# Which weight blocks a recurrent attention loop streams: one key block kept, a sixth output block streamed

## The chip, the core and the metric

The kernel runs on one core of a Trainium2 chip. The metric is the device time of the whole kernel in microseconds. Three runs before the change took 2378.48, 2380.43 and 2387.71 us; the median is 2380.43. The profiled execution spans 2380.4 us at a mean granted TensorE clock of 0.97.

## The reference

Two independent parts are computed and joined along the last axis. Part B is a long convolution over 2048 positions and 1024 channels; nothing of it is touched here. Part A is an attention layer with a recurrent memory, and it fixes the order of the work:

```python
for s in range(n_seg):                       # 64 segments of 32 positions
    h = concat([mem, x[:, 32*s:32*s+32]])    # 8 memory rows + 32 rows, 1024 wide
    q, k, v = h @ Wq, h @ Wk, h @ Wv         # 32 heads of 128
    p = softmax(mask(q @ k.T * scale))
    o = (p @ v) @ Wo
    mem = o[:, :8]                           # the next segment needs it
    outs.append(o[:, 8:])
```

Each segment needs the memory that the segment before it made, so the 64 steps run one after the other. Each of the four weights has 1024 x 4096 values, 8 MB in bf16: 32 MB together[...].

## The kernel before

Part B and all of part A that doesn't depend on the memory run first, up to about 719 us. Then `part_a` runs its 64 steps, and a last stage of some 60 us makes the rows that could be put off (lines 557 to 575).

Weights are cut into 64 blocks of 128 x 2048 values, 512 KB each. The key weight has two halves `("k", 0)` and `("k", 1)` of eight blocks, one for each 128 rows of the contraction; query and value likewise. The output weight has sixteen blocks `("o", 0)` to `("o", 15)` of two heads each. I write (k,1,3) for block 3 of the second key half.

The blocks are of three kinds. 45 are resident in SBUF from the first step on. Two, (k,0,7) and (o,15), are parked in PSUM and copied into pieces each step (`KEPT`, `fetch`). The other 17 are streamed: read from DRAM again in each step. `STREAM` and `STREAM_O` say which, and everything else follows from these two lines: `streamed_copies` makes a DRAM copy (`WD_...`) of each of them, and `RESIDENT` (line 209) takes the rest.

A step uses the blocks in a fixed order, in `quads` (line 349) for q, k and v and in `oproj` (line 448) for the output: k0, q0, k1, q1, v0, v1, each from 0 to 7, then o from 0 to 15. Attention for the first 16 heads runs between the v0 and v1 blocks, and the second half's between (o,6) and (o,8). I call the matmuls of one block a unit; back to back, a unit takes about 0.22 us.

`unit(key)` gives the block for a unit. For a streamed one it takes the next of `SLOTS = 5` buffers in turn and issues the load from SyncE's queue:

```python
between.pop(key, lambda: None)()
...
t_ = wst.tile([128, 2048], BF16, name="wst", tag="w%d" % (loads[0] % SLOTS))
loads[0] += 1
nc.sync.dma_start(out=t_[:], in_=WD[key][:])
```

[...]A load waits there until the matmuls of the block that was in this buffer five loads earlier are done[...]. `between` puts a few other transfers into the same queue, each just ahead of a streamed block's load: `pk` (192 KB, line 312) ahead of (q,0,1), the two stores of the step before (64 KB each, lines 327 and 331) ahead of (k,1,3), and `xt` (48 KB, line 317) ahead of (o,13).

Of the kernel before, what the change touches and what calls it, by code (L numbers as in the profile page):

```python
# [21 lines left out]

STREAM = {("k", 0): (0, 5), ("q", 0): (1, 5), ("k", 1): (0, 3), ("q", 1): (0, 4), ("v", 0): (0, 4), ("v", 1): (0, 4)}
STREAM_O = (0, 4, 8, 11, 13)

KEPT = {("k", 0, 7): (("B", 0, 512), ("C", 512, 512), ("A", 1024, 512), ("F", 1536, 256), ("L", 1792, 256)),
        ("o", 15): (("B", 0, 512), ("C", 512, 512), ("E", 1024, 512), ("F", 1536, 256), ("L", 1792, 256))}
# [19 lines left out]
def streamed_keys():  # L49
    return [key for key in [(m, t, kc) for (m, t), kcs in STREAM.items() for kc in kcs] + [("o", u) for u in STREAM_O]]  # L50

# [1390 lines left out]
```

## Time and profile before

| part of the span | us | TensorE busy, us | DMA share |
|---|---|---|---|
| part B and projections, to 719 us | 719.0 | 595.2 | |
| first step, with the last resident loads | 41.8 | 26.8 | 1.01 |
| 62 steps, 760.8 to 2294.9 us | 1534.1 | 1297.7 | 1.00 |
| last step and last stage | 85.5 | 75.5 | 0.53 |

A step ends where the new memory has been copied into `hT` (line 552); from 760.8 to 2294.9 us that happens 62 times more, every 24.74 us. A streamed block is read in full in every step, so the loop moves 17 x 512 KB and the small transfers each time.

In the profile PE is TensorE, DVE VectorE, ACT ScalarE and SP SyncE; "SPq" is SyncE's queue, whose rows are issues of DMAs, not the transfers themselves. DMA share is the mean busy share of the core's 16 DMA engines. `wst<-WD_k` is a load of a streamed key block, `acc<-wst,hT` the matmuls that use one in line 349 and `pp<-wst,oT` those in line 448. "Idle before" is the time that an engine stood still ahead of an instruction, and the name after the arrow is what ended it.

### The profile page before, as it was taken

How to read it: one execution, taken by the hardware profiler on the slowest of the kernel's cores; microseconds unless marked ns; L12 is line 12 of the kernel's file. 1: busy time of each engine (PE TensorE's matmuls, PEld its weight loads, DVE VectorE, ACT ScalarE, POOL GpSimd, SP SyncE). 2: the span in 40 equal slices, each digit the busy share in tenths (PEclk: the TensorE clock that was granted, in tenths of full speed). 3: DMA queues.
4: the chain of work that ended last, by engine and by line, in shares of the span. 5: the costliest groups of instructions: out<-in, count | busy, mean ns of one | idle time of the engine just before them, and what ended most of it. 6: DMA issues, size and time to landing. Idle time of an engine off the chain costs nothing.

```text
span 2380.4 us, 78429 instructions
## 1 busy us (share of the span) xinstructions
PE 1995.2 (84%) x33798; PEld 1176.3 (49%) x33798; DVE 1472.6 (62%) x3164; ACT 974.1 (41%) x1596; POOL 359.1 (15%) x614
## 2 busy tenths in 40 slices
PE   1699999779997888888888888888888888888889
PEld 1366665668883444444444444444444444444444
DVE  9599999999973545555454554544545545454550
ACT  6699999713342323232332332323323233332330
POOL 2144354573220000000000000000000000000001
PEclk6799999989997999999999999999999999999999
DMA  6786885684479999999999999999999999999993
GB/s 160 187 238 194 249 229 155 185 254 167 143 278 376 387 387 369 382 388 380 379 362 371 384 381 380 372 380 365 377 362 384 371 385 385 389 374 372 390 373 111
DMA packets 379680, 759.08 MB, mean 319 GB/s; under 512 B 121704, under 2 KB 213000, under 8 KB 377284
## 3 DMA queue, kind: packets, MB, share of 16 engines
q1 hardware_dynamic: 365268, 714.08, 83.4%
q0 software_dynamic: 14064, 39.99, 5.1%
q8 instruction: 264, 4.33, 0.7%
q14 instruction: 84, 0.69, 0.1%
HBM read 699.16 MB, written 67.88 MB: 322 GB/s over the span
## 4 chain that ended last, share of the span: by engine, by line
PE 37%; DMA 30%; DVE 22%; ACT 7%; issue 4%; SPq 1%; DVEq 0%; ACTq 0%; POOL 0%; POOLq 0%
DMA wst<-WD_k 15%; PE acc L349 10%; DMA wst<-WD_o 8%; PE yp L1237 4%; PE hps L1005 4%; PE pp L448 3%; DMA wst<-WD_q 3%; DMA wst<-WD_v 3%; PE pe L569 2%; PE pro L158 2%; DVE nr L1066 2%; PE ups L864 2%; PE pa L1035 2%; PE tr L360 1%; DVE sc L395 1%
## 5 line engine op out<-in xcount | busy, mean ns | idle before, releaser
L349 PEld LDWEIGHTS <-hT 128*32 128x32 bf16 x12352 | 326.0, 96 | 466.4 <-issue 243.5
L349 PE MATMUL acc<-wst,hT 128*32 128x512 bf16 x3072 | 312.0, 390 | 158.3 <-DMA wst<-WD_k 61.6
L349 PE MATMUL acc<-W,hT 128*32 128x512 bf16 x5120 | 399.4, 383 | 0.0
L355 ACT CAST ev<-acc 128x512 bf16<-128x512 f32 x384 | 225.1, 586 | 399.9 <-PE acc L349 395.1
L448 PEld LDWEIGHTS <-oT 128*32 128x32 bf16 x8192 | 202.8, 96 | 109.4 <-issue 82.6
L282 DVE TENSOR_SCALAR piece<-keep 128x256 int32<-128x256 int32 (+1 forms) x640 | 190.5, 363 | 50.7 <-PE pp L448 31.2
L387 DVE TENSOR_REDUCE mx<-sc 128x8 f32<-128x320 f32 x128 | 62.4, 488 | 244.3 <-PE sc L380 244.2
L448 PE MATMUL pp<-W_o,oT 128*32 128x256 bf16 x4096 | 182.0, 275 | 5.9 <-DMA W_o<-in_A_Wo_dram 5.9
L361 DVE COPY KT<-tr 128x512 bf16<-128x512 bf16 x64 | 27.2, 425 | 258.0 <-PE tr L360 258.0
L368 POOL COPY KT<-pk 128x128 bf16<-128x128 bf16 x128 | 37.9, 296 | 801.1 <-PE sc L380 443.8
L349 PE MATMUL acc<-MF,hT 128*32 128x512 bf16 x2048 | 157.3, 381 | 0.0
L448 PE MATMUL pp<-wst,oT 128*32 128x256 bf16 x2560 | 128.2, 277 | 32.2 <-DMA wst<-WD_o 23.2
L361 ACT COPY QT<-tr 128x512 bf16<-128x512 bf16 x128 | 75.0, 586 | 189.7 <-PE tr L360 188.8
L435 ACT CAST oT<-pv 128x512 bf16<-128x512 f32 x128 | 75.0, 586 | 167.2 <-PE pv L421 165.4
L321 POOL COPY hT<-xt 128x192 bf16<-128x192 bf16 x63 | 22.0, 349 | 723.6 <-DMA xt<-XTd 426.1
L158 PE MATMUL pro<-xTl,wsl 128*128 128x512 bf16 x512 | 120.2, 385 | 5.2 <-ACT xTl L102 5.2
L1005 PEld LDWEIGHTS <-MF 128*128 128x128 bf16 x1024 | 102.5, 100 | 30.3 <-issue 8.8
L389 ACT ACTIVATE sc<-sc 128x320 f32<-128x320 f32 x128 | 54.0, 422 | 152.7 <-DVE sc L388 149.9
L1005 PE MATMUL hps<-KT,MF 128*128 128x256 bf16 x720 | 94.4, 284 | 14.6 <-DVE x L1180 11.5
L360 PEld LDWEIGHTS <-ev 128*128 128x128 bf16 x1024 | 57.9, 98 | 96.5 <-issue 66.3
L1237 PE MATMUL yp<-Bt,MI 128*128 128x256 bf16 x680 | 102.8, 273 | 0.8 <-ACT yb L1253 0.8
L360 PE MATMUL tr<-a_ident,ev 128*128 128x128 bf16 x1024 | 101.8, 222 | 0.0
(313 smaller groups left out, 3791.1 us busy)
## 6 DMA issues: line engine op xcount, KB each, us to landing
wst<-WD_o SPq DMA_DIRECT2D x320, 512.0 KB
wst<-WD_k SPq DMA_DIRECT2D x256, 512.0 KB
wst<-WD_q SPq DMA_DIRECT2D x256, 512.0 KB
wst<-WD_v SPq DMA_DIRECT2D x256, 512.0 KB
Ud<-ux POOLq DMA_DIRECT2D x16, 1024.0 KB, 5.8
uq<-Ud SPq DMA_DIRECT2D x32, 512.0 KB
pk<-PKd SPq DMA_DIRECT2D x64, 192.0 KB
wsl<-in_A_Wk_dram SPq DMA_DIRECT2D x16, 512.0 KB
```

What stands on the lines that cost most here:

```text
L158: nc.tensor.matmul(a[:], lhsT=w[:, kc, 128 * j:128 * j + 128], rhs=xTl[:, kc, :, :].rearrange("p s k -> p (s k)"), start=(kc == 0), stop=( ...
L282: nc.vector.tensor_scalar(out=out.bitcast(I32), in0=in_.bitcast(I32), scalar1=0, scalar2=None, op0=ALU.bitwise_or)
L349: nc.tensor.matmul(a[32 * g:32 * g + 32, o_:o_ + rhs.shape[1]], lhsT=hT[:, kc, :], rhs=rhs, start=(kc == 0), stop=(kc == KC - 1), tile_pos ...
L355: nc.scalar.copy(out=q[:], in_=a[:])
L360: nc.tensor.transpose(out=p[:, i, hl, :, :].rearrange("p a b -> p (a b)"), in_=q[:, 128 * hl:128 * hl + 128], identity=ident[:])
L361: eng(out=dst, in_=p[:, i, :, :, :])
L387: nc.vector.tensor_reduce(out=mx[:], in_=sc, axis=AX.X, op=ALU.max)
L389: nc.scalar.activation(out=sc, in_=sc, func=ACT.Exp, scale=scale)
L435: nc.scalar.copy(out=o[:], in_=p[:].rearrange("p a (g q) -> p a g q", g=4))
L448: nc.tensor.matmul(po[32 * qt:32 * qt + 32, :], lhsT=oT[:, h % 4, (h % 16) // 4, :], rhs=columns(w, 1024 * hh + 256 * qt, 256)[0][1], star ...
L1005: pe.matmul(s_[r][half][:, cs, :], lhsT=MF[:, kc, 4 * rr + mc, cs, :], rhs=rhs, start=(i == 0 and mc == 0), stop=(i == 1 and mc == 3), ski ...
L1237: pe.matmul(yp[:, b, :], lhsT=m_[:, b, cs, kc, :], rhs=Bt[:, kc, j, half, c_, :], start=(kc == 0 and cs == 0 and half == 0), stop=(kc == 3 ...
```

## The change

One key block less and one output block more is streamed, and the output blocks are chosen anew. (k,1,0) becomes resident. Of the output blocks, 0, 4, 8, 11 and 13 were streamed; now 0, 3, 6, 8, 11 and 13 are, so that (o,4) becomes resident. It is meant to spread the reads of streamed blocks differently over a step: the stretch with (q,0,1), (q,0,5), (k,1,0) and (k,1,3) close together gets one fewer, the output projection one more.

```diff
-STREAM = {("k", 0): (0, 5), ("q", 0): (1, 5), ("k", 1): (0, 3), ("q", 1): (0, 4), ("v", 0): (0, 4), ("v", 1): (0, 4)}
-STREAM_O = (0, 4, 8, 11, 13)
+STREAM = {("k", 0): (0, 5), ("q", 0): (1, 5), ("k", 1): (3,), ("q", 1): (0, 4), ("v", 0): (0, 4), ("v", 1): (0, 4)}
+STREAM_O = (0, 3, 6, 8, 11, 13)
```

Still 17 blocks are streamed and 45 resident. In order of use the streamed blocks are:

| | load 1 to 5 | load 6 to 11 | load 12 to 17 |
|---|---|---|---|
| before | k00 k05 q01 q05 k10 | k13 q10 q14 v00 v04 v10 | v14 o0 o4 o8 o11 o13 |
| after | k00 k05 q01 q05 k13 | q10 q14 v00 v04 v10 v14 | o0 o3 o6 o8 o11 o13 |

Each load takes the buffer of the block five places earlier, counted on over the end of a step. So from (k,1,3) to the end of the step every streamed block sits in the buffer one place on, and is released by another use than before.

## The prediction

> **What bounds the kernel now.** I read the stretches first, to find the stage that counts. Columns: stretch, length, busy time of each engine, clock, DMA share, GB/s.
>
> ```profile
> 719.00:760.80 41.80, 26.84 (x422) 12.27 (x414) 15.54 (x41) 9.06 (x18) 1.66 (x4) 0.76 1.01 380
> 760.80:2294.90 1534.10, 1297.65 (x26412) 680.24 (x26412) 805.33 (x2232) 479.42 (x930) 58.42 (x186) 0.99 1.00 378
> 2294.90:2380.40 85.50, 75.54 (x680) 35.76 (x680) 19.54 (x48) 11.12 (x20) 9.40 (x9) 0.99 0.53 196
> ```
>
> The 62 steps from 760.8 to 2294.9 us take 24.74 us each; everything else stays as it is. In them the DMA share is 1.00 and TensorE is busy 85%, so two limits lie close together. Adding the times of TensorE's units in a step without the idle time that a DMA ended gives 22.4 us. Adding median packet times (159 ns for 4096 bytes, 8 packets per queue engine and block) gives 17 x 1.28 = 21.8 us for the blocks and 1.1 us for pk, xt and the stores: 22.9 us. The measured step is 1.8 us above the larger. Packets stretched beyond 159 ns fill the DMA share to 1.00, so that share alone doesn't prove a full queue.
>
> Then the waits, for who pays those 1.8 us (waiter, releaser, total us, times, longest), with SyncE's queue below:
>
> ```profile
> PE acc L349 <- DMA wst<-WD_k: 61.6, 78, 2.2
> PE acc L349 <- DMA wst<-WD_q: 51.9, 109, 1.6
> SPq L268 <- PE acc L349: 406.5, 577, 2.7
> SPq L268 <- PE pp L448: 106.2, 259, 1.6
> ```
>
> TensorE waits for blocks, and SyncE, which issues them, waits for TensorE to free one of the five buffers: a closed loop. Summing the idle time ahead of each unit over 60 steps gives, per step: (k,1,3) 0.87 us, (q,0,1) 0.57, (q,0,5) 0.24, (k,1,0) 0.08, (o,13) 0.33, others 0.15; 2.24 in all. The timeline of one step shows the loop (start, duration, instruction, idle before it and who ended that):
>
> ```profile
> 1500.94 0.32 SPq L327 DMA_DIRECT2D OLd<-ob  x1
> 1501.25 0.40 PE L349 MATMUL acc<-wst,hT 128*32 128x512 bf16 x4 [0.33 <-PE tro L551]
> 1501.31 0.55 SPq L331 DMA_DIRECT2D out_dram<-ob  x1
> ...
> 1501.96 0.47 SPq L268 DMA_DIRECT2D wst<-WD_k  x1
> ...
> 1509.60 0.40 PE L349 MATMUL acc<-wst,hT 128*32 128x512 bf16 x4 [2.13 <-DMA wst<-WD_k]
> ...
> 1515.19 0.40 PE L349 MATMUL acc<-wst,hT 128*32 128x512 bf16 x4
> ...
> 1518.51 0.40 PE L349 MATMUL acc<-wst,hT 128*32 128x512 bf16 x4
> ...
> 1519.74 0.40 PE L448 MATMUL pp<-wst,oT 128*32 128x256 bf16 x8
> ...
> 1523.98 0.39 PE L448 MATMUL pp<-wst,oT 128*32 128x256 bf16 x8
> ...
> 1524.41 0.39 PE L448 MATMUL pp<-wst,oT 128*32 128x256 bf16 x8
> ```
>
> From the top: two stores, with (k,0,0) used between them, the issue of (k,1,3) after (k,0,0) is done and the stores are out, and its use 7.6 us later, 2.13 of them waited. Below are the uses of (v,0,4), (v,1,4), (o,0), (o,11) and (o,13).
>
> [...]here the 48 KB xt took at least 3.6 us from issue to landing, so I use landings of the trace. [...]folding all steps over each other, the trace has 396 to 405 GB/s in microseconds 5 to 10 of a step and 330 to 341 in 18 and 19. The queue can run faster than its mean.[...]
>
> **The change, part by part.** (k,1,0) is no longer streamed, (o,4) becomes resident, (o,3) and (o,6) are streamed. A step still moves 17 blocks of 512 KB, with the same matmuls. At 390 and 275 ns matmuls don't care where their weights lie: zero for TensorE. The first step still loads 11 resident and 17 streamed blocks: zero. The last stage reloads 7 output blocks instead of 6: one transfer of 1.3 us, hidden, as the tail's DMA share is 0.53 and TensorE runs nine resident blocks there first; zero.
>
> What moves is which use frees the buffer for which load. With five buffers, load n is issued when block n-5 is done with. I call the time on TensorE from one use to the other, DMA waits left out, the window. It has to hold the use of 0.40 us and the time from issue to landing. That I averaged from the trace's semaphore counts over 59 steps: (o,4) 6.0 us, (o,8) 6.0, (o,11) 5.7, (o,13) 5.7, (k,1,3) 6.4; the shortest of any load was 4.0.
>
> Before, the short windows are (k,0,0) to (k,1,3) 5.3 us, (o,8) to (q,0,1) 5.6, (o,11) to (q,0,5) 5.95 and (v,1,4) to (o,13) 6.0. These four are where TensorE waits: the view explains before. After:
> - (k,1,3) takes the buffer of (o,13): window 7.5. Its issue still stands behind the stores, 0.8 us after the step's start, but the queue ahead of it is one block shorter: 6.4 - 1.3 = 5.1 us to landing, at 5.9. Its use is at 5.3 plus the waits at (q,0,1) and (q,0,5), 0.8: 6.1. Its wait and that of (k,1,0), 0.95, fall to about 0.1.
> - (q,0,1) and (q,0,5) keep windows and waits: zero.
> - (o,3) takes that of (v,0,0): 6.5 - 0.4 = 6.1 against 6.0: 0.1.
> - (o,6) takes that of (v,0,4): 1515.19 to 1521.07, 5.9 - 0.4 = 5.5 against 6.0: 0.5. Behind it TensorE now idles 0.28 us a step for VectorE's softmax (lines 403 and 406), which doesn't depend on (o,6): 0.25 of it is hidden.
> - (o,11) takes that of (v,1,4): 1518.51 to 1523.98, 5.5 - 0.4 = 5.1 against 5.7: 0.6, of which the 0.5 at (o,6) lies in the same window: 0.1 to 0.15.
> - (o,13) takes that of (o,0): 1519.74 to 1524.41, 4.7 - 0.4 = 4.3 against 5.7: 1.4, less the 0.5 ahead: 0.9. Now 0.33.
> - Every other load has a window of 6.3 us or more: zero.
>
> The sum per step: before 0.95 + 0.34 = 1.29. After 0.1 + 0.1 + (0.5 - 0.25) + 0.15 + 0.9 = 1.5. That is +0.2 us. The gaps between issues also grow, to 2.1 us from (q,0,5)'s use to (k,1,3)'s, so the DMA engines run dry a little more often; I put 0.05 on it. 0.25 x 63 = 16 us: **2396 us**.
>
> Unknown is how long (o,13) needs: its queue holds (o,8), (o,11) and xt, as now, so I take 5.7. At the shortest, 4.0, it waits for nothing and the step gets shorter; at 6.4, as for (k,1,3), it waits 1.6.
>
> **Rivals.**
> 1. *Faster: the key half was the only knot.* For it: (k,1,3) has the largest wait, and (o,8) lands 1.6 us ahead of its use. If loads late in the step land in 4.6 us, as the quickest of them do, (o,6) and (o,11) wait for nothing and (o,13) 0.3 as before: 0.85 us saved. Spaced at the 1.33 us at which blocks land in mid-step, transfers alone need 17 x 1.33 + 1.2 = 23.8, so at most 0.9 could go. Half of it is given back at (q,0,1) and (q,0,5), whose queue comes later: 0.4 x 63 = 25 us, 2355. Against it: the average landing is 5.7, not 4.6.
> 2. *No change: bytes pace the step.* The share is 1.00 and the bytes are the same, so the waits only move: 2380. Against it: the rate dips to 330.
> 3. *Slower by more.* (o,13)'s wait pushes its own release, and thereby the issue of (k,1,3), and SyncE holds (k,1,3) behind stores that now come later. If (o,13) takes 6.0 us to land, as (o,4) and (o,8) do, it waits 1.2 and the step loses 0.55: 0.55 x 63 = 35 us, 2415.
>
> **How the numbers follow.** My forecast (2385 to 2405) 0.40, rival 3 0.14, rival 2 0.22, rival 1 0.24. Slower by over 0.5% (above 2392): all of rival 3 and most of my forecast, 0.50. Faster by over 0.5% (below 2368.5): rival 1 without its small gains, 0.24. The same: 0.26. The range takes in rival 2, rival 3 up to a little past its middle and rival 1's upper half: 2358 to 2418.
>
> **What would show it.** Right: idle time at line 349 for WD_k falls from 61.6 us to below 15, that at line 448 for WD_o grows from 23.2 to 85 or more, most of it ahead of the thirteenth output block; VectorE's lines 403 and 406 end fewer TensorE waits; DMA bytes unchanged. Wrong: WD_o's wait stays below 50 us, which rival 1 needs, or (k,1,3) still waits, held by the stores. The forecast fails if late loads land sooner once fewer are queued ahead.

## The result and the profile after

The changed kernel takes 2442.29 us (median of 4 runs, 2433.43 to 2455.54), the one before 2383.07 us in the same comparison. The ratio is 1.0253, 95% interval 1.0201 to 1.0306: 59 us slower. The profiled execution of the changed kernel is the longest of its four, 2453.8 us at a mean clock of 0.935; the other three ran at 0.954 to 0.958, the profiled one of before at 0.970. So figures of its profile overstate the loss: its span is 73 us longer than that of the profile before, not 59.

The three parts of the part-A work in the changed kernel (stretch, length, busy time of PE, PEld, DVE, ACT and POOL, clock, DMA share, GB/s):

```profile
719.00:764.10 45.10, 28.31 (x422) 13.12 (x414) 16.11 (x43) 9.08 (x17) 1.66 (x4) 0.74 0.98 361
764.10:2362.80 1598.70, 1359.01 (x26412) 700.40 (x26412) 809.50 (x2234) 479.37 (x930) 58.42 (x186) 0.94 0.98 362
2362.80:2453.80 91.00, 79.53 (x674) 36.63 (x680) 18.98 (x48) 11.12 (x20) 9.62 (x9) 0.93 0.52 187
```

The 62 steps grew by 64.6 us, 1.04 us each. The first step took 3.3 us more at nearly the same clock (0.74, before 0.76), the last stretch 5.5 us more at 0.93 in place of 0.99. Two things stand in the middle row. TensorE is busy for 1359.01 us with the 26412 matmuls that took 1297.65 before: 0.99 us a step more for the same work. And the clock is 0.94, not 0.99.

Who waits for whom in the changed kernel, TensorE first, then SyncE's queue (total us, times, longest), and below it two rows of before:

```profile
PE pp L448 <- DMA wst<-WD_o: 128.6, 169, 2.2
PE acc L349 <- DMA wst<-WD_q: 19.2, 49, 0.9
PE acc L349 <- DMA wst<-WD_k: 13.0, 21, 1.2
SPq L327 <- ACT ob L554: 181.9, 63, 4.4
```

```profile
PE pp L448 <- DMA wst<-WD_o: 23.2, 38, 1.4
SPq L327 <- ACT ob L554: 63.2, 62, 2.4
```

The waits for key blocks fell from 61.6 to 13.0 us and those for output blocks rose from 23.2 to 128.6, as forecast. Summed as in the prediction, per step: (o,13) 1.02 us, (o,6) 0.52, (o,11) 0.31, (k,1,3) 0.17, (q,0,1) 0.14, (q,0,5) 0.10; with the rest 2.6 in all, against 2.24 before. So waits grew by 0.35 us a step, and the steps by three times that. (The other idle time of TensorE shrank by 0.3 us a step.) The last row is SyncE's wait at the store of line 327 for the result that it stores. It grew from 63.2 to 181.9 us, and the prediction counted it only as a delay of (k,1,3).

One step's end shows what happens to the clock. The first two lines are stretches of 3.4 us that follow one another, the rest is the timeline in them:

```profile
2331.60:2335.00 3.40, 1.56 (x44) 0.97 (x39) 0.85 (x4) 0.00 (x0) 0.35 (x1) 0.99 1.00 370
2335.00:2338.40 3.40, 2.99 (x26) 1.27 (x30) 1.58 (x6) 0.54 (x2) 0.00 (x0) 0.51 1.02 394
```

```profile
2331.89 0.40 PE L448 MATMUL pp<-wst,oT 128*32 128x256 bf16 x8 [0.19 <-DMA wst<-WD_o]
...
2333.73 0.40 PE L448 MATMUL pp<-wst,oT 128*32 128x256 bf16 x8 [1.22 <-DMA wst<-WD_o]
...
2335.01 0.64 PE L551 MATMUL tro<-a_ident,ob 128*128 128x128 bf16 x2 [0.45 <-DVE ob L546]
...
2336.36 1.52 PE L349 MATMUL acc<-W_k,hT 128*32 128x512 bf16 x12
```

The waits at (o,11) and (o,13) lie close ahead of a step's end, where TensorE stands still anyway for the copy of the result. In the first stretch it is busy 1.56 of 3.40 us. In the next the clock is 0.51, and the three units (k,0,1) to (k,0,3) take 1.52 us; in the step of before that the prediction shows, the same twelve take 0.83 us:

```profile
1501.47 0.83 PE L349 MATMUL acc<-W_k,hT 128*32 128x512 bf16 x12
```

The same shows over the whole loop. In all twelve traces the granted clock is either full or half, and every stretch between two changes lasts a whole number of 3.413 us. So I cut the loop into windows of that length, aligned with the changes, and took those at full clock:

| busy share of TensorE in a window | before: windows, halved after | changed: windows, halved after | all twelve traces: windows, halved after |
|---|---|---|---|
| below 0.5 | 5, 5 | 26, 25 | 133, 123 |
| 0.5 to 0.6 | 13, 2 | 25, 14 | 190, 64 |
| 0.6 or more | 423, 0 | 362, 0 | 4884, 5 |

The border is not sharp, and the five in the last row all belong to one run, the one with a pause below. There are 7 spells of half clock in the loop before, 24 us together, and 39 after, 188 us; 36 of these 39 begin within 4 us of a step's end, as do 5 of the 7. The spells of before last 3.4 us, those of the changed kernel 3.4 or 6.8, one or two windows. No window has to be idle throughout: being busy for less than half of it was enough in 123 of 133. What sets the clock no trace shows; the table says only how often half clock followed such a window.

### The profile page after: what moved, and what is told of

It reads as the page before. It is cut to its first block, busy times and chain, and to the rows that moved or that the text cites. A ratio compares the mean times of both kernels' runs of the same rounds, so it can differ in the third digit from the quotient of the medians.

```text
span 2453.8 us, 78406 instructions
## 1 busy us (share of the span) xinstructions
PE 2060.7 (84%) x33773; PEld 1198.5 (49%) x33798; DVE 1476.3 (60%) x3164; ACT 974.2 (40%) x1596; POOL 359.6 (15%) x614
## 4 chain that ended last, share of the span: by engine, by line
PE 42%; DMA 35%; DVE 8%; issue 8%; ACT 5%; POOL 2%; SPq 0%; ACTq 0%; DVEq 0%; POOLq 0%
PE acc L349 23%; DMA wst<-WD_o 16%; DMA wst<-WD_q 6%; DMA wst<-WD_v 4%; PE pp L448 3%; DMA wst<-WD_k 3%; PE pe L569 2%; PE tr L360 2%; PE pro L158 2%; DVE nr L1066 2%; DMA out_dram<-uu 2%; PE ups L864 2%; PE pa L1035 2%; ACT ev L355 1%; DMA KT<-Kd 1%
## 5 line engine op out<-in xcount | busy, mean ns | idle before, releaser
L349 PEld LDWEIGHTS <-hT 128*32 128x32 bf16 x12352 | 343.5, 101 | 392.7 <-issue 198.9
L349 PE MATMUL acc<-W,hT 128*32 128x512 bf16 x5376 | 468.5, 398 | 0.9 <-DMA W<-in_A_Wv_dram 0.9
L349 PE MATMUL acc<-wst,hT 128*32 128x512 bf16 x2816 | 302.2, 411 | 72.7 <-DMA wst<-WD_q 19.2
L448 PEld LDWEIGHTS <-oT 128*32 128x32 bf16 x8192 | 208.9, 98 | 227.3 <-issue 198.5
L448 PE MATMUL pp<-wst,oT 128*32 128x256 bf16 x3072 | 159.1, 284 | 138.0 <-DMA wst<-WD_o 128.6
L448 PE MATMUL pp<-W_o,oT 128*32 128x256 bf16 x4096 | 189.0, 282 | 5.5 <-DMA W_o<-in_A_Wo_dram 5.4
L547 ACT CAST ob<-pp 128x128 bf16<-128x128 f32 x64 | 17.0, 266 | 287.5 <-DVE ob L546 287.5
```

The lines of the kernel that those rows point to most:

```text
L349: nc.tensor.matmul(a[32 * g:32 * g + 32, o_:o_ + rhs.shape[1]], lhsT=hT[:, kc, :], rhs=rhs, start=(kc == 0), stop=(kc == KC - 1), tile_pos ...
L448: nc.tensor.matmul(po[32 * qt:32 * qt + 32, :], lhsT=oT[:, h % 4, (h % 16) // 4, :], rhs=columns(w, 1024 * hh + 256 * qt, 256)[0][1], star ...
```

## The experiments

Two theories at first. **Clock**: beyond the longer waits, their place costs, since they share a window with the idle end of a step and the clock is halved. **Waits**: it is all waits, and the slow clock falls into time that TensorE would wait anyway. A third joined them from the SyncE row: a **hole** in the queue of loads, a time in which no load is issued.

| run | us | ratio to before | 95% interval | spells at half clock in the loop |
|---|---|---|---|---|
| changed | 2442.3 | 1.0253 | 1.0201 to 1.0306 | 39 |
| extra matmuls ahead of (o,13) | 2421.5 | 1.0152 | 1.0117 to 1.0188 | 8 |
| extra matmuls ahead of (q,1,5) | 2527.2 | 1.0602 | 1.0567 to 1.0637 | 44 |
| sixth block in v0 | 2405.5 | 1.0091 | 1.0065 to 1.0118 | 15 |
| o10 and o14 | 2426.8 | 1.0188 | 1.0154 to 1.0222 | 15 |
| stores behind (k,1,3) | 2411.9 | 1.0111 | 1.0085 to 1.0137 | 29 |
| the same and extra matmuls | 2385.8 | 1.0005 | 0.9986 to 1.0025 | 4 |
| before, stores behind (k,1,3) | 2365.1 | 0.9919 | 0.9896 to 0.9943 | 6 |
| before, (k,1,4) for (k,1,3) | 2351.7 | 0.9873 | 0.9845 to 0.9901 | 9 |
| before, pause ahead of (o,13) | 2412.4 | 1.0117 | 1.0100 to 1.0134 | 12 |
| before, pause filled with work | 2391.9 | 1.0027 | 1.0010 to 1.0044 | 4 |

The spells are counted in one profiled execution of each.

### Keeping TensorE busy where it waits, and where it doesn't

```diff
+        def warm(n):
+            if s + 1 < NS:
+                f = ps_acc.tile([128, 512], F32, name="fill", tag="acc")
+                for _ in range(n):
+                    nc.tensor.matmul(f[:], lhsT=ident[:], rhs=W_res["v", 0, 1][:, 0:512], start=True, stop=True)
...
             for u in us:
+                if u == 13:
+                    warm(4)
                 w = unit(("o", u))
```

The twin calls `warm(4)` in `quads` ahead of (q,1,5).

> The changed kernel with four extra matmuls (128x512, result unused) on TensorE just ahead of the unit of (o,13), in all steps but the last: they fill about 0.86 us of the wait for that block with work and move no data. Clock theory (the waits at (o,11) and (o,13) lie together near the end of a step, the clock of TensorE is halved after a stretch in which it was busy too little, and that costs some 40 of the 60 us): stretches at half clock in the loop fall from 39 to under 12 and the time falls by 25 to 45 us, to 1.006 to 1.014 of before, although TensorE has more to do. Waits theory (all 60 us are waits for blocks; the halved clock only falls into time in which TensorE would wait anyway): no gain, 1.025 to 1.035 of before.

> The changed kernel with the same four extra matmuls at another place, ahead of the unit of (q,1,5), where TensorE doesn't wait for blocks. Clock theory: stretches at half clock stay at 30 or more, no time is won, and up to 0.5 us a step is lost: 1.025 to 1.040 of before. Waits theory: the same as for the matmuls ahead of (o,13), so both runs come out within 0.5% of each other.

Ahead of (o,13), more work made the kernel 21 us faster; the same work ahead of (q,1,5) made it 85 us slower. The waits theory wanted both alike, and no gain. The clock by slice of the span, in tenths, first of the changed kernel, then with the matmuls ahead of (o,13):

```profile
PEclk6799999899998999999989999999999999988999
```

```profile
PEclk9999999899998999999999999999999999999999
```

The low first two digits lie ahead of part A's loop and stand in the profile of before as well. In the second, the loop (from the thirteenth digit on) shows no low slice past the first step. TensorE was busy for 1362.1 us in the loop, with the extra matmuls, against 1359.0 without them: its other work took some 50 us less.

Both sizes were missed. The gain is below the 25 to 45 us expected; the four matmuls are work too, and may delay a step in which the wait is shorter than their 0.86 us (an estimate: 4 x 0.215, from start to start of 128x512 matmuls in line 158 of the trace of before). The loss ahead of (q,1,5), 1.0602, is far above the 1.040 that the clock theory allowed. There the 0.86 x 63 = 54 us of work came on top, which an account by waits alone would allow as well. The loop was also at half clock for 262 us in place of 188, as (o,13) then waited 1.35 us. So it is the gain of the first run that speaks for the clock.

### The same change with the waits put elsewhere

```diff
-STREAM = {... ("k", 1): (3,), ... ("v", 0): (0, 4), ...}
-STREAM_O = (0, 3, 6, 8, 11, 13)
+STREAM = {... ("k", 1): (3,), ... ("v", 0): (0, 3, 6), ...}
+STREAM_O = (0, 4, 8, 11, 13)
```

> The changed kernel, but the read taken out of the second key half goes to the first value half (blocks 0, 3 and 6) and the output blocks are those of before (0, 4, 8, 11, 13). Windows: (v,0,3) 5.4 us, (o,13) 6 us as before. Clock theory: (k,1,3) waits under 0.2 us, waits of about 0.3 us each turn up at (v,0,3), (v,0,6) and (o,4), all in all some 0.3 us a step more than before, but spread, so that stretches at half clock stay under 15: 1.005 to 1.014 of before. Waits theory with the loss in removing the key block itself: as slow as the changed kernel, 1.02 or more. If the output half alone was to blame and the rest is a gain: 0.99 or less.

```diff
-STREAM_O = (0, 3, 6, 8, 11, 13)
+STREAM_O = (0, 3, 6, 8, 10, 14)
...
-            between["o", 13] = lambda: put_xt(load_xt(s + 1))
+            between["o", 10] = lambda: put_xt(load_xt(s + 1))
```

> The changed kernel with output blocks 10 and 14 streamed in place of 11 and 13 (and xt read ahead of (o,10)). It spreads the waits at the end of the output projection: about 0.3 us at (o,10) and 0.5 at (o,14) in place of 0.3 and 1.0 at (o,11) and (o,13). Clock theory: under 25 stretches at half clock and 1.008 to 1.018 of before. Waits theory: waits per step 0.1 to 0.2 us shorter than in the changed kernel and no more than 12 us won: 1.020 to 1.025.

With the sixth read in v0, waits were 2.3 us a step, in many places, with 15 spells of half clock, one too many for the clock theory: 1.0091, inside its interval. So taking (k,1,0) out was not what cost 59 us. The windows did not tell all places: (o,13) waited 0.74 us, not 0.33 as before, and (v,1,0) 0.28.

With (o,10) and (o,14) there were as few spells although waits were the longest of all, 2.7 us a step: 1.0188, between the two intervals. But this run has a cost of its own. In the last step the load of (o,14) stands behind eleven loads for the last stage, and TensorE waits 15.8 us for it, the longest wait of this row:

```profile
PE pp L448 <- DMA wst<-WD_o: 121.9, 194, 15.8
```

In the other runs the last streamed block is (o,13), whose load goes out ahead of them. Without this wait the run would be at about 1.012, by this estimate inside the clock theory's 1.008 to 1.018 and below the waits theory's 1.020.

### The hole in the queue

In the changed kernel SyncE issues the load of (q,0,5) 3.4 us ahead of a step's start and the next, (k,1,3), 0.8 us after it: 4.3 us with no load between, while one takes 1.3 to transfer. The buffer of (k,1,3) comes free with (o,13), but the load stands behind two stores that wait for the step's result. In the step shown above the matmuls of (o,13) end at 2334.13 us, the stores go out at 2335.61 and 2336.02, the load at 2336.68. In the traces of both kernels this load comes behind the two stores, as the program has it, in all 62 steps of the loop. Before, the load of (k,1,0) went out 1.6 us ahead of the start. The edit lets the load go first:

```diff
-    between = {}
+    between, behind = {}, {}
...
         nc.sync.dma_start(out=t_[:], in_=WD[key][:])
+        behind.pop(key, lambda: None)()
         return t_
...
-            between["k", 1, 3] = lambda: stores(s - 1, ob)
+            behind["k", 1, 3] = lambda: stores(s - 1, ob)
```

> The changed kernel with the two stores of the step before issued just behind the load of (k,1,3) instead of just ahead of it. In the changed kernel SyncE issues nothing from 3.4 us ahead of a step's start to 0.8 us after it, although the buffer of (k,1,3) comes free with (o,13), and the transfer rate falls to 290 to 350 GB/s in microseconds 1 to 5 of a step. Hole theory (this hole in the queue is most of what the change costs beside the clock): the load goes out some 2 us sooner, the rate there stays above 355, the step gets 0.2 to 0.35 us shorter, and the time is 1.014 to 1.020 of before; stretches at half clock stay above 25, as the waits at (o,11) and (o,13) stay. Windows theory (only the short windows of (o,6), (o,11) and (o,13) count; (k,1,3) itself waits 0.2 us): no more than 0.1 us a step, 1.022 to 1.028.

> Both remedies on the changed kernel: the stores behind the load of (k,1,3), and four extra matmuls ahead of the unit of (o,13). If clock and hole are two separate costs, they add: 21 us from the clock and 15 to 20 from the hole, 1.005 to 1.011 of before. If one was a part of the other: 1.013 to 1.017, as with the extra matmuls alone. What is then left above before is the longer waits in the output projection.

> The kernel before with the stores behind the load of (k,1,3). There this load also waits for the buffer of (k,0,0), so it goes out only 0.25 us sooner. Hole theory: before, (k,1,0) was issued 1.6 us ahead of the step's start and filled the hole; the gain is small, 0.05 to 0.15 us a step, 0.995 to 1.000 of before. If SyncE's order costs as much here as in the changed kernel: 0.992 or less.

SyncE's queue around a step's start, without and with the edit (start, duration of the issue):

```profile
1300.33 2.61 SPq L268 DMA_DIRECT2D wst<-WD_q  x2
1305.55 0.32 SPq L327 DMA_DIRECT2D OLd<-ob  x1
1305.99 0.55 SPq L331 DMA_DIRECT2D out_dram<-ob  x1
1306.64 0.42 SPq L268 DMA_DIRECT2D wst<-WD_k  x1
```

```profile
1284.90 0.32 SPq L268 DMA_DIRECT2D wst<-WD_q  x1
1286.28 0.32 SPq L268 DMA_DIRECT2D wst<-WD_k  x1
1287.72 0.32 SPq L328 DMA_DIRECT2D OLd<-ob  x1
1288.09 0.56 SPq L332 DMA_DIRECT2D out_dram<-ob  x1
```

In the first, the load for `WD_k` is last; in the second it leaves 1.4 us ahead of the stores. Over all steps it goes out 2.6 us sooner. Folded over all steps, the rate in microseconds 1 to 5 of a step was 289 to 353 GB/s in the changed kernel and is 374 to 400 with the edit. The wait of SyncE for the stores' result is back to where it was before the change:

```profile
SPq L328 <- ACT ob L555: 70.5, 63, 2.4
```

The edit won 30 us, more than the 12 to 26 that 1.014 to 1.020 stood for. Not all of it is the queue: spells fell from 39 to 29, and TensorE's busy time in the loop's profile from 1359.0 to 1336.6 us, so a part of the gain is likely the clock's. Extra matmuls ahead of (o,13) on top of it won another 26 us. The two gains add, and together they went past the 1.005 expected at best: 1.0005.

But the kernel before gained 19 us from the same edit, 0.9919. That is past the 0.995 expected at best by the hole theory, and at the 0.992 that stood for the rival, by which SyncE's order costs as much here as in the changed kernel. Its waits for key blocks fell from 0.97 to 0.68 us a step. There too the load of (k,1,3) stood behind the stores, and it left 0.26 us sooner. Whether that or the 128 KB of the stores, no longer ahead of it, was worth 0.3 us a step, no run separates.

So 19 us were lost already before the change. What the change added is less certain: 30 - 19 = 11 us lies inside the noise of these four medians (by their intervals, 15 us either way), and the fewer spells may account for it. With the extra matmuls in both, where spells are few (8 and 4), the edit won 36 us; 36 - 19 = 17 us, by the intervals 5 to 27, and up to 7 of it can be the clock.

### The clock in the kernel before, with no block moved

Both runs hold TensorE for about 1.1 us ahead of (o,13). One of them lets it idle in between:

```diff
+                z = work.tile([128, 512], BF16, name="z", tag="E")
+                nc.scalar.copy(out=z[:], in_=f[:])
+                nc.tensor.matmul(f[:], lhsT=ident[:], rhs=z[:], start=True, stop=True)
```

This stands behind one matmul of `warm(1)`; the twin calls `warm(5)`.

> The kernel before, streams untouched, with a pause of about 1.1 us ahead of the unit of (o,13) in all steps but the last: one extra matmul, a copy of its result on ScalarE (0.59 us) and a second extra matmul that needs the copy, so that TensorE stands still for some 0.75 us of it. Clock theory: the pause comes on top of the wait of 0.33 us and the idle time at the end of a step, so the clock is halved 25 times or more in the loop (7 before), and the run is at least 12 us longer than its twin with the same time filled by matmuls. Rival (the halved clock costs nothing, since it falls into time that TensorE would wait for blocks anyway): both within 6 us of each other.

> The twin of the pause: the kernel before with five extra matmuls (1.1 us of work) at the same place, ahead of the unit of (o,13). Clock theory: under 8 stretches at half clock; the time is 10 to 45 us above before, as far as the 1.1 us isn't taken up by waits for blocks, and at least 12 us below the run with the pause. Rival: as the run with the pause.

The pause was 20 us slower than its twin, as the clock theory has it, with every run of the twin (2380.7 to 2399.1 us) below the pause's shortest, 2408.1. The twin cost 9 us, just under the 10 expected. But the pause brought 12 spells of half clock, not 25, and 9 of them came after windows in which TensorE was busy 0.59 to 0.63 of the time, at or above the border seen in the table. Its idle part measured 0.73 us, so with two matmuls of 0.22 it held TensorE 1.17 us, against 1.08 of five matmuls: 0.09 x 63 = 6 us of the 20 are its length. The loop was at half clock for 41 us against 14: 27 us more, in which at most half, 14 us, is lost. The two can make up the 20, but with a count that I missed by half, this pair supports the theory rather than sizing it.

### A version that beats both

```diff
-... ("k", 1): (0, 3), ...
+... ("k", 1): (0, 4), ...
...
-        if s:
-            between["k", 1, 3] = lambda: stores(s - 1, ob)
...
+        if s:
+            stores(s - 1, ob)
         QT0 = new_qt()
```

> The kernel before with (k,1,4) streamed in place of (k,1,3), the stores just ahead of its load; all else as before. Its use lies 0.67 us later on TensorE, behind the transposes, so the shortest window of the kernel before, 5.3 us, becomes 5.9. Windows theory: the wait of 0.87 us there falls to some 0.3, about a third of it comes back at (q,1,4), whose window shrinks, and the step gets 0.1 to 0.25 us shorter: 0.993 to 0.998 of before. If bytes alone pace the step: 0.998 to 1.002.

One block moved by one place in the kernel before, with the stores kept just ahead of its load: 2351.7 us, 32 us less, and past the expected 0.993. The stretch of its loop:

```profile
760.50:2264.80 1504.30, 1302.63 (x26416) 677.08 (x26420) 808.32 (x2233) 478.85 (x930) 57.99 (x186) 0.99 1.01 385
```

```profile
PE acc L349 <- DMA wst<-WD_q: 54.3, 113, 2.1
PE pp L448 <- DMA wst<-WD_o: 26.3, 50, 2.2
PE acc L349 <- DMA wst<-WD_k: 19.7, 34, 1.5
```

A step takes 24.26 us, and the rate is 385 GB/s against 378. TensorE's busy time is as before; the wait for key blocks fell from 61.6 to 19.7 us, and only some 5 us came back in the rows for query and output blocks. In the changed kernel it fell further, to 13.0, and the wait for query blocks by 33 us, but the 105 us more for output blocks outweigh both.

## Why the prediction was wrong

The direction was right and the size was not: 16 us forecast, 59 measured, and 2442.3 lies outside the range of 2358 to 2418. Step by step:

- *What bounds the kernel, and the windows.* Right in the main. The waits came where the windows put them. Forecast and measured, us per step: (o,3) 0.1 and 0.07; (o,6) 0.5 and 0.52; (o,11) 0.15 and 0.31; (o,13) 0.9 and 1.02; (k,1,3) 0.1 and 0.17. Landings were taken as 5.1 us for (k,1,3) and 5.7 for (o,13), and were 5.0 and 6.25 on average. The idle time for VectorE behind (o,6) fell from 0.28 to 0.04, so the 0.25 that I took as hidden was hidden.
- *(q,0,1) and (q,0,5) keep their waits: zero.* Wrong, in the kernel's favour: 0.81 became 0.24. A wait at (o,13) lies inside both their windows, and the prediction, which let one wait hide another in the output projection, did not do so here. That the waits in all grew by 0.35 us, not far from the forecast 0.2, is therefore luck: this miss covers the larger waits elsewhere.
- *"390 and 275 ns matmuls don't care where their weights lie: zero for TensorE."* This is the step that failed. Where the weights lay made little difference: in the loop of before, matmuls with resident blocks took 379 to 403 and 273 ns on average. But it put the change in TensorE's own work at nothing, and where TensorE idles changed it: at half clock the same matmuls took 0.99 us a step longer in the profiled execution. Not all of that is time lost: on the medians, keeping TensorE busy ahead of (o,13) was worth 21 us alone and 26 us with the stores behind the load. The trace of before held the evidence: 7 spells of half clock, each behind a window with a busy share below 0.6.
- *(k,1,3)'s issue behind the stores, priced as that block's own wait, 0.1.* Mis-sized. The wait was 0.17, but no load was issued for 4.3 us, which holds up all blocks behind it. The term for this was the 0.05 us for engines that run dry. It looks at the wrong gap: the 2.1 us lie between the uses of (q,0,5) and (k,1,3), which free the buffers of (v,0,4) and (v,1,0), and not between the loads of (q,0,5) and (k,1,3) themselves, which the stores hold 4.3 us apart. What the term should have been, the runs tell only roughly, 11 to 17 us or 0.17 to 0.27 us a step, with the noise given above.
- *The waits in the output projection.* With the stores behind the load in both, and the clock kept up, the changed kernel is at 2385.8 and the one before at 2365.1: 21 us. It includes what the extra matmuls themselves cost, and no run has them in the kernel before with its stores behind, so the forecast's 16 us for this part is within what these runs can tell.
- *First step and last stage: zero each.* In the profiled execution they took 3.3 and 5.5 us more. With the extra matmuls ahead of (o,13) both are as before; with the stores behind as well they are not. The cause stays open.

The clock's 26, the queue's 11 and these 21 us add up to the 58 or 59 measured. This confirms nothing: the three are differences between the same medians taken along one chain of edits, so they must add up. Along the other order of the edits, the clock is worth 21 us and the queue 36 - 19 = 17. The clock's part is clear of noise in both orders; the queue's is not in the first; and the last 21 us are what is left over, put down to longer waits but tested by no run.

Rival 3 came closest in the number. It named the store queue as a way to lose more, but had the cost come through a longer wait at (o,13), of 1.2 us, and put it at 2415; (o,13) waited 1.02. Rival 1 needed the waits for `WD_o` below 50 us; they were 128.6. Rival 2, bytes alone, falls with the two versions of before: both move the same bytes and are 19 and 32 us faster.

## What to carry to other kernels

Before moving a wait, look at what idle time lies within some 3.4 us of its new place, the length of the windows in these traces. In the kernel before, (k,1,3) waited 0.87 us a step away from other idle time, and the loop had 7 spells of half clock. In the changed kernel (o,11) and (o,13) waited 1.3 us together next to some 0.8 us at the step's end (0.45 ahead of line 551 and 0.33 ahead of line 349 in the lines shown), and it had 39. With a ring of buffers, list for every load the time from the use that frees its buffer to its own use: the shortest such windows told where most of the waits fell, though not all. And price a load that stands behind a store not by the wait for that load alone: moving it ahead of the stores won 30 and 19 us where its own wait was 0.17 and 0.87 us a step.

## What the runs showed of the hardware

In these twelve traces TensorE's clock was halved after 123 of 133 windows of 3.41 us in which TensorE was busy for less than half, after a third of those between 0.5 and 0.6, and almost never above. No single wait is needed that fills such a window: the longest idle time in the changed kernel's loop was 2.2 us. Shorter ones add up: in the stretch from 2331.60 us, shown above, they are 0.19 and 1.22 us for blocks and 0.45 for the step's result, and the clock was halved behind it. At full clock a unit of four matmuls in line 349 takes 0.216 us from its start to that of the next, at half clock 0.427 (medians of the changed kernel's trace). Useless work could then pay: ahead of (o,13), four extra matmuls per step made the kernel 21 us faster.

Blocks landed, averaged by their place in the step, 5.6 to 7.1 us after their issue in the kernel before and 5.0 to 7.2 in the changed one, though the packets of one take 1.3 us. That holds even for loads with an emptier queue ahead: (k,1,3) in the changed kernel took 5.0 us on average and 3.7 at the least.
